# Summing Strassen-Winograd products over 128 partitions instead of 64, in a gated feed-forward layer behind polysketch attention

## The chip, the cores and the metric

The kernel runs on one core of one Trainium2 chip. A core has TensorE (PE: matrix products; PEld in a profile is its loading of weights), VectorE (DVE), ScalarE (ACT), GpSimd (POOL) and SyncE (SP), which here only issues transfers. The metric is the device time of one execution, in microseconds (us); lower is better. All data are float32. The matrices come in as float64, seen by the kernel as pairs of 32-bit words, and are narrowed to float32 on the chip.

## What is computed

```python
def phi(x):                      # q, k, v: (4, 4, 1088, 32); S1, S2: (8, 32)
    a = np.einsum('rd,bhsd->bhsr', S1, x)
    b = np.einsum('rd,bhsd->bhsr', S2, x)
    return np.einsum('bhsi,bhsj->bhsij', a, b).reshape(*x.shape[:-1], 64)
q_p, k_p = phi(q), phi(k)
kv = np.einsum('bhsf,bhsd->bhfd', k_p, v)
z = np.sum(k_p, axis=2)
x = einsum('bhsf,bhfd->bhsd', q_p, kv) / (einsum('bhsf,bhf->bhs', q_p, z)[..., None] + 1e-6)
x = x.transpose(0, 2, 1, 3).reshape(4352, 128)
gate = 1.0 / (1.0 + np.exp(-(x @ w_gate)))      # w_gate, w_val: (128, 1536)
out = (gate * (x @ w_val)) @ w_out              # w_out: (1536, 128)
```

## The kernel before

The 4352 tokens of the feed-forward layer are cut into nine chunks: eight of 512 tokens (0 to 7) and one of 256 (chunk 8). A chunk takes twelve *waves* (chunk 8 takes six, each of two column blocks of 256 tokens). A wave, `w1`, multiplies 128 columns of `w_gate` and of `w_val` with the chunk's tokens into a double PSUM buffer `wave` (two of them in turn), and issues ScalarE's sigmoid (`sg`). The product of the two halves, `g`, is VectorE's `glu`; it is emitted at the start of the next wave's turn. The instructions' order on each engine is the order in which the Python code emits them.

One turn of the loop in `slot` is called a *slot* here: `glu` of the wave before, then one piece of work from the list `moe["late"]`, then all products with `w_out` whose due slot (`todo`) has come, then the next wave with its sigmoid. Attention for batches 1 to 3 is spread between the slots by a plan written out by hand (`plan`), so that its steps (`turn_k`, `turn_q`, `begin`, `outer`, `sum_z`, `kv_all`, `qmult`, `ndt`, `weights_z`, `parts`) come at numbered waves; batch 0 runs at the start of the kernel, with `warm` products on constants between its steps to fill TensorE. `begin` ends with transfers that spread a small matrix `cq` over partitions by way of DRAM (`dq`); `parts` needs what they bring (`denj` reads `b` and others).

Chunk 0 and chunk 8 multiply with `w_out` plainly (`w2`, `w2_end`, output tile `moeout`). Chunks 1 to 7 (`fast`) use a scheme of seven products for each 2 x 2 block product: two neighbouring waves are a pair; the blocks are two column blocks of the pair by two halves of 256 tokens (`HALF`), against two row blocks of `w_out` by two halves of 64 output columns. GpSimd makes four differences of `g` for each pair (`token_sums`, tile `tsum`, `t[0]` to `t[3]`; `t[0]` after the even wave, the other three after the odd one), and weight sums `ws` once (`weight_sums`). Each of the seven products has 64 output rows and 256 columns, so two lie side by side on the 128 columns of TensorE's array: `lo` (output partitions 0 to 63) and `hi` (64 to 127). `w2_a` issues four of the seven into the PSUM bank `acc0`, `w2_b` three into `acc1`, each accumulated over the chunk's six pairs. `w2_a` is due three slots after the pair's odd wave, `w2_b` four; the last pair of chunk 7 one slot sooner (`early`).

After the sixth pair the seven accumulated products are combined into the chunk's 128 x 512 output. They lie on both halves of the partitions[...]; so ScalarE copies the `hi` half of a bank to partitions 0 to 63 (tile `other`, variable `e`), and VectorE sums on 64 partitions into `res` (variable `r`). The first copy and sum follow the last `w2_a` at once (L473, L475); the other sums, two transposes of 64 x 512 (L514) and the store are pieces of `moe["late"]`, one a slot (two a slot in chunk 8). `store` issues its four or more transfers on SP. `acc0` and `acc1` have one buffer each: the next chunk's first product into a bank waits until all readers of the old sums are through. `w2_end` uses `acc0` for the last chunk's output, and `store_end` copies that to two `o_end` tiles which share the two buffers of `o_sb`.

Of the kernel before, what the change touches and what calls it, by code (L numbers as in the profile page):

```python
# [8 lines left out]
F32 = mybir.dt.float32  # L9
# [3 lines left out]
ALU = mybir.AluOpType  # L13
# [3 lines left out]
P = 128  # L17
# [3 lines left out]
def kernel(  # L21
# [12 lines left out]
    nc = tc.nc  # L34
# [6 lines left out]
    NJ = DFF // P  # L41
# [7 lines left out]
    TCH = 512  # L49
    tok_chk = [(o, min(TCH, NTOK - o)) for o in range(0, NTOK, TCH)]  # L50
# [3 lines left out]
    sbA = ctx.enter_context(tc.tile_pool(name="sbA", bufs=2))  # L54
# [131 lines left out]
    HALF = TCH // 2  # L186
# [157 lines left out]

    xT = const.tile([P, NTOK], F32, tag="xT")

    moe = {"sum": -1, "ci": 0, "w": 0, "n": 0, "ready": 0, "acc": None, "gate": None, "todo": [], "late": []}

    def fast(ci):
        return 0 < ci < len(tok_chk) - 1 and tok_chk[ci][1] == TCH  # L350
# [14 lines left out]
    def token_sums(g, t, odd):  # L365
        def sub(u, in0, in1):
            nc.gpsimd.tensor_tensor(out=t[:, u], in0=in0, in1=in1, op=ALU.subtract)  # L367

        if not odd:
            sub(0, g[:, 0, HALF:], g[:, 0, :HALF])  # L370
            return
        sub(2, g[:, 1, HALF:], t[:, 0])
        sub(3, t[:, 2], g[:, 1, :HALF])
        sub(1, g[:, 1, HALF:], g[:, 0, HALF:])

    def product(out, lhsT, rhs, start, stop):
        nc.tensor.matmul(  # L377
            out=out, lhsT=lhsT, rhs=rhs, start=start, stop=stop, skip_group_check=True
        )
# [34 lines left out]
    def w2(ci, j0, jn, g):  # L414
        if j0 == 0:
            moe["sum"] = ci
            moe["acc"] = pso.tile([P, TCH], F32, tag="acc0", name="moeout")
        for jj in range(jn):
            j = j0 + jj
            for d in (slice(0, P),) if j < NJ - 2 else (slice(0, 64), slice(64, P)):  # L420
                nc.tensor.matmul(  # L421
                    out=moe["acc"][d],
                    lhsT=w_sb[:, 2, j, d],
                    rhs=g[:, jj],
                    start=(j == 0),
                    stop=(j == NJ - 1),
                )
        if j0 + jn == NJ:
            o_sb = sbA.tile([P, 2, TCH // 32, 32], F32, tag="o_sb", name="o_sb")[:, 0]
# [27 lines left out]

    fst = {}

    def w2_a(ci, i, g, t):  # L460
        if i == 0:
            moe["sum"] = ci
            fst["a"] = pso.tile([P, TCH], F32, tag="acc0", name="prod")
        lo, hi = fst["a"][:64], fst["a"][64:]
# [12 lines left out]

    def add(out, in0, in1, op=ALU.add):
        nc.vector.tensor_tensor(out=out, in0=in0, in1=in1, op=op)  # L479

    def twice(x):
        return bass.AP(tensor=x.tensor, offset=x.offset, ap=[list(x.ap[0]), [0, 2], [1, HALF]])

    def ends(r, u, step):
        x = r[:, u]
        return bass.AP(
            tensor=x.tensor, offset=x.offset, ap=[list(x.ap[0]), [step * HALF, 2], [1, HALF]]
        )

    def w2_b(ci, i, g, t):  # L490
        if i == 0:
            fst["b"] = pso.tile([P, TCH], F32, tag="acc1", name="prod")
        lo, hi = fst["b"][:64], fst["b"][64:]
        w, first, last = w_sb[:, 2], i == 0, i == NJ // 2 - 1
        p5 = (lo[:, :HALF], ws[:, 0, i], t[:, 0], first, last)
        p4 = (hi[:, :HALF], w[:, 2 * i + 1, 64:], t[:, 3], first, last)
        p7 = ((hi if i % 2 else lo)[:, HALF:], ws[:, 2, i], t[:, 1], False, i >= NJ // 2 - 2)
        for p in (p4, p5, p7) if i % 2 else (p5, p4, p7):
            product(*p)
        if last:  # L500
            e, r = fst["e"], fst["r"]
            nc.scalar.copy(out=e[:, 1], in_=hi.rearrange("p (u x) -> p u x", u=2))
            o_sb = sbA.tile([P, 2, TCH // 32, 32], F32, tag="o_sb", name="o_sb")

            def fifth_seventh():
                add(ends(r, 2, 3), twice(lo[:, :HALF]), ends(r, 2, 2))
                add(r[:, 0], lo[:, HALF:], e[:, 1, 1])

            def last_sums():
                add(r[:, 3], r[:, 4], e[:, 1, 0], op=ALU.subtract)  # L510
                add(r[:, 3:5], ends(r, 3, 2), twice(r[:, 0]))

            def turned(d):
                nc.vector.transpose(  # L514
                    out=o_sb[:64, d].rearrange("p t x -> p (t x)"),
                    in_=r[:, 1 + 2 * d : 3 + 2 * d].rearrange("p u x -> p (u x)"),
                )

            def turn_store():
                turned(1)  # L520
                store(ci, lambda g4: o_sb[32 * (g4 % 2) : 32 * (g4 % 2) + 32, g4 // 2])

            moe["late"] += [fifth_seventh, last_sums, lambda: turned(0), turn_store]

    def w1():

# [45 lines left out]
        def glu():  # L572
            g = pair[:, odd]
            todo = moe["todo"]
            if jn == 2:
                nc.vector.tensor_tensor(  # L576
                    out=g.rearrange("p (j u s y) -> p j y u s", j=2, u=2, y=4),
                    in0=wv[:, 1].rearrange("p (j y u s) -> p j y u s", j=2, u=2, y=4),
                    in1=sg.rearrange("p (j y u s) -> p j y u s", j=2, u=2, y=4),
                    op=MUL,  # L580
                )
            else:
                nc.vector.tensor_tensor(out=g, in0=wv[:, 1], in1=sg, op=MUL)  # L583
            if not fast(ci):
                lag = 4 if ci else 2
                part = (ci, j0, jn, g.rearrange("p (j t) -> p j t", j=jn))
                todo.append((n + lag, lambda: (w2_end if ci else w2)(*part)))
                return
            if not odd:
                moe["t"] = raw.tile([P, 4, HALF], F32, tag="w_in", name="tsum")  # L590
            token_sums(pair, moe["t"], odd)
            if odd:
                part = (ci, j0 // 2, pair, moe["t"])
                early = ci == len(tok_chk) - 2 and j0 == NJ - 1
                todo.append((n + 3 - early, lambda: w2_a(*part)))
                todo.append((n + 4 - early, lambda: w2_b(*part)))

        moe["gate"] = glu
        moe["w"] += 1
# [10 lines left out]
    def slot(group, waves, behind=None):  # L610

        if group is not None:
            group()
        todo = moe["todo"]
        for _ in range(waves):
            more = moe["ci"] < len(tok_chk)
            if more and sum(tok_chk[moe["ci"]]) > moe["ready"]:
                break
            glu()
            for _ in range(2 if moe["ci"] >= len(tok_chk) - 1 else 1):  # L620
                if moe["late"]:
# [781 lines left out]
```

## Time and profile before

| | us |
|---|---|
| median of 3 runs (lowest, highest) | 292.83 (292.31, 293.69) |
| the profiled execution: its own time | 296.02 |
| its span, first to last instruction | 294.1 |
| TensorE busy, share of the span | 288.8, 98% |
| VectorE busy | 186.5, 63% |
| ScalarE busy | 93.7, 32% |
| GpSimd busy | 160.6, 55% |

The page of a profile gives busy times, groups of equal instructions by source line with their mean duration, and the chain of work that ended last. Further views are used here: the timeline (start and length in us, engine, line, operation, tile written and tiles read, shapes), tables of busy time by stretches of the span, and a list of waits. An item `[1.11 <-PE wave L540]` says that the engine had been idle for 1.11 us before the instruction and that TensorE's work of line 540 ended this. A float32 matrix product is recorded as two passes, so counts of matmuls are twice those in the code. Most lines of the profile are those of small helpers: L377 is every one of the seven products, L367 every difference on GpSimd, L479 every sum on VectorE.

### The profile page before, as it was taken

To read this page: it belongs to the slowest core of one execution; us is meant where nothing else is said; L and a number is where in the kernel's file an instruction comes from. 1 tells how busy PE (TensorE), PEld (TensorE's weight loads), DVE (VectorE), ACT (ScalarE), POOL (GpSimd) and SP (SyncE) were. 2 spreads that over 40 slices of the span, in tenths; PEclk is the share of its full clock that TensorE was granted. 3 is DMA by queue.
4 is the path that set the end of the run, shared out by engine and by line. 5 is a ranking of instruction groups with operands and counts; after the bars stand their busy time and mean duration, and the time that the engine had idled before them with its cause. 6 is when DMAs were issued, how large, how long until landed. Compare 5 with 4: busy or idle time off the path is not lost.

```text
span 294.1 us, 5762 instructions
## 1 busy us (share of the span) xinstructions
PE 288.8 (98%) x2264; PEld 156.6 (53%) x2264; DVE 186.5 (63%) x316; ACT 93.7 (32%) x172; POOL 160.6 (55%) x222
## 2 busy tenths in 40 slices
PE   8989999999999999999999999999999999999995
PEld 3543433355455455545555555554555555555895
DVE  5778789885656766677556696667436423552482
ACT  3386542321324222323224222323223223322321
POOL 2266544796535657655456498555456565646300
PEclk9999999999999999999999999999999999999999
DMA  7993613295640168416000474202000200020003
GB/s 219 347 336 68 150 39 125 74 180 137 186 97 0 19 163 159 133 50 177 12 0 2 129 174 106 37 0 38 1 0 2 36 2 0 0 31 7 0 4 54
DMA packets 28890, 24.23 MB, mean 82 GB/s; under 512 B 18560, under 2 KB 24064, under 8 KB 28864
## 3 DMA queue, kind: packets, MB, share of 16 engines
q1 hardware_dynamic: 25808, 21.95, 30.1%
q10 hardware_dynamic: 3056, 1.92, 2.3%
q8 instruction: 18, 0.29, 0.4%
q14 instruction: 8, 0.07, 0.1%
HBM read 20.60 MB, written 3.26 MB: 81 GB/s over the span
## 4 chain that ended last, share of the span: by engine, by line
PE 89%; DMA 7%; SPq 1%; DVE 0%; issue 0%; ACT 0%; DVEq 0%
PE wave L540 55%; PE prod L377 20%; DMA bq<-dq 5%; PE moeout L421 4%; PE moeout L447 2%; PE warm L297 1%; PE kps L673 1%; SPq L844 1%; PE nps L1258 1%; DMA s_in<-in_S_dram 1%; PE kvz L892 1%; PE cqps L819 1%; DMA dq<-cq 1%; DMA b<-dq 1%; PE denj L1021 0%; PE dps L1063 0%
## 5 line engine op out<-in xcount | busy, mean ns | idle before, releaser
L540 PE MATMUL wave<-xT,w_sb 128*64 128x512 f32 (+3 forms) x820 | 210.6, 566 | 0.0
L540 PEld LDWEIGHTS wave<-xT,w_sb 128*64 128x64 f32 (+1 forms) x820 | 85.4, 140 | 63.2 <-issue 51.0
L548 ACT ACTIVATE sg<-wave 128x512 f32<-128x512 f32 x102 | 60.9, 597 | 171.1 <-PE wave L540 163.2
L583 DVE TENSOR_TENSOR g<-wave,sg 128x512 f32<-128x512 f32 x96 | 65.9, 686 | 76.3 <-ACT sg L548 75.0
L367 POOL TENSOR_TENSOR tsum<-g 128x256 f32<-128x256 f32 x84 | 67.9, 810 | 29.7 <-DVE g L583 29.6
L367 POOL TENSOR_TENSOR tsum<-g,tsum 128x256 f32<-128x256 f32 x42 | 34.2, 814 | 57.8 <-DVE g L583 57.6
L377 PE MATMUL prod<-tsum,ws 128*64 128x256 f32 x252 | 62.8, 381 | 0.0
L377 PEld LDWEIGHTS prod<-tsum,ws 128*64 128x64 f32 x252 | 31.2, 137 | 16.0 <-issue 11.8
L377 PE MATMUL prod<-g,w_sb 128*64 128x256 f32 x168 | 34.7, 381 | 0.0
L367 POOL TENSOR_TENSOR tsum<-tsum,g 128x256 f32<-128x256 f32 x42 | 32.7, 779 | 3.3
L377 PE MATMUL prod<-tsum,w_sb 128*64 128x256 f32 x84 | 25.3, 383 | 0.0
L377 PEld LDWEIGHTS prod<-g,w_sb 128*64 128x64 f32 x168 | 16.0, 136 | 17.5 <-issue 14.7
L377 PE MATMUL prod<-g,ws 128*64 128x256 f32 x84 | 25.0, 379 | 0.0
L117 POOL TENSOR_TENSOR head<-head,tail 128x384 int32<-128x384 int32 (+1 forms) x10 | 9.9, 987 | 13.9 <-DVE head L111 12.6
L377 PEld LDWEIGHTS prod<-g,ws 128*64 128x64 f32 x84 | 11.5, 137 | 3.7
L421 PE MATMUL moeout<-g,w_sb 128*128 128x512 f32 (+1 forms) x28 | 12.5, 603 | 0.0
L377 PEld LDWEIGHTS prod<-tsum,w_sb 128*64 128x64 f32 x84 | 10.8, 137 | 3.0 <-issue 2.2
L872 DVE TENSOR_TENSOR qp<-qp,bq 128x1152 f32<-128x1152 f32 (+1 forms) x7 | 9.4, 1344 | 4.6 <-DMA a<-dq 4.6
L752 DVE TENSOR_TENSOR kp<-kab 128x1152 f32<-128x1152 f32 (+2 forms) x10 | 10.9, 1101 | 0.0
L576 DVE TENSOR_TENSOR g<-wave,sg 128x512 f32<-128x512 f32 x6 | 6.7, 1121 | 4.6 <-ACT sg L548 4.6
L479 DVE TENSOR_TENSOR res<-prod,other 64x512 f32<-64x512 f32 (+1 forms) x14 | 7.6, 544 | 3.1 <-DMA a<-dq 1.6
L514 DVE STREAM_TRANSPOSE o_sb<-res 64x512 f32<-64x512 f32 x14 | 9.6, 688 | 0.0
(129 smaller groups left out, 209.6 us busy)
## 6 DMA issues: line engine op xcount, KB each, us to landing
qp<-dq SPq DMA_DIRECT2D x7, 576.0 KB
bq<-dq SPq DMA_DIRECT2D x14, 288.0 KB
kq<-in_k_dram SPq DMA_DIRECT2D x3, 544.0 KB
kq<-in_q_dram SPq DMA_DIRECT2D x3, 544.0 KB
w_in<-in_moe_w_out_dram SPq DMA_DIRECT2D x6, 256.0 KB
w_in<-in_moe_w_gate_dram SPq DMA_DIRECT2D x5, 256.0 KB
w_in<-in_moe_w_val_dram SPq DMA_DIRECT2D x5, 256.0 KB
v<-in_v_dram SPq DMA_DIRECT2D x8, 144.0 KB
```

The lines of the kernel that those rows point to most:

```text
L117: nc.gpsimd.tensor_tensor(out=head, in0=head, in1=tail, op=ALU.add)
L367: nc.gpsimd.tensor_tensor(out=t[:, u], in0=in0, in1=in1, op=ALU.subtract)
L377: nc.tensor.matmul(out=out, lhsT=lhsT, rhs=rhs, start=start, stop=stop, skip_group_check=True)
L421: nc.tensor.matmul(out=moe["acc"][d], lhsT=w_sb[:, 2, j, d], rhs=g[:, jj], start=(j == 0), stop=(j == NJ - 1),)
L479: nc.vector.tensor_tensor(out=out, in0=in0, in1=in1, op=op)
L514: nc.vector.transpose(out=o_sb[:64, d].rearrange("p t x -> p (t x)"), in_=r[:, 1 + 2 * d : 3 + 2 * d].rearrange("p u x -> p (u x)"),)
L540: nc.tensor.matmul(out=wv[d, which, jj * tw + o : jj * tw + o + tp], lhsT=w_sb[:, which, j0 + jj, d], rhs=xT[:, t0 + o : t0 + o + tp], sta ...
L548: nc.scalar.activation(out=sg, in_=wv[:, 0], func=ACTF.Sigmoid)
L576: nc.vector.tensor_tensor(out=g.rearrange("p (j u s y) -> p j y u s", j=2, u=2, y=4), in0=wv[:, 1].rearrange("p (j y u s) -> p j y u s", j ...
L583: nc.vector.tensor_tensor(out=g, in0=wv[:, 1], in1=sg, op=MUL)
L752: eng.tensor_tensor(out=KP[b][:, pi, j0:j1].rearrange("p j m (i l) -> p (j m) i l", i=R), in0=bass.AP(tensor=a0.tensor, offset=a0.offset, ...
L872: nc.vector.tensor_tensor(out=q0, in0=q0, in1=half(BQ[b], n), op=MUL)
```

## The change

- The seven products are dealt out anew. `w2_a` takes `t[2]` and `t[1]` in place of one product on `g` and of one on `t[2]`; the product of `g` with the second row block moves to `w2_b`. The signs and the order of GpSimd's differences are changed to suit.
- The sums run over 128 partitions. ScalarE makes seven copies of 64 x 256 for each chunk instead of two of 64 x 512, in both directions between the halves (`cross`). They are put on a list, `moe["copies"]`, and emitted in `slot` behind the next wave, hence behind its sigmoid. Six read PSUM; one reads a sum, `r[64:, 0]`.
- VectorE makes five sums (four of 128 x 256, one of 64 x 256) and one transpose of 128 x 512 for each chunk. All of them are late pieces: first `shared`, with the two sums that read `acc0` (the second reads the first's result), a slot after the last `w2_a`; then `first_half`, one sum, and `turn_store`, which stores.
- The first pair of chunk 1 has its `w2_a` and `w2_b` due one slot later (`behind`); the last pair of chunk 7 is no longer due one sooner.
- The warm product behind the transpose of the sketches, at the start of the kernel, has 128 columns instead of 64. `o_sb` is half as large.

```diff
         sub(2, g[:, 1, HALF:], t[:, 0])
-        sub(3, t[:, 2], g[:, 1, :HALF])
         sub(1, g[:, 1, HALF:], g[:, 0, HALF:])
+        sub(3, g[:, 1, :HALF], t[:, 2])
...
     def w2_a(ci, i, g, t):
...
         product(lo[:, :HALF], w[:, 2 * i, :64], g[:, 0, :HALF], first, last)
-        product(hi[:, :HALF], w[:, 2 * i + 1, :64], g[:, 1, :HALF], first, last)
+        product(hi[:, :HALF], ws[:, 1, i], t[:, 2], first, last)
         product(lo[:, HALF:], ws[:, 3, i], g[:, 1, HALF:], False, last)
-        product(hi[:, HALF:], ws[:, 1, i], t[:, 2], False, last)
+        product(hi[:, HALF:], ws[:, 2, i], t[:, 1], False, last)
         if last:
-            e = fst["e"] = raw.tile([P, 2, 2, HALF], F32, tag="w_in", name="other")[:64]
-            r = fst["r"] = raw.tile([P, 6, HALF], F32, tag="w_in", name="res")[:64]
-            nc.scalar.copy(out=e[:, 0], in_=hi.rearrange("p (u x) -> p u x", u=2))
-
-            add(ends(r, 1, 3), twice(lo[:, :HALF]), e[:, 0])
-            moe["late"] += [lambda: add(r[:, 2], lo[:, HALF:], r[:, 4])]
+            e = fst["e"] = raw.tile([P, 4, HALF], F32, tag="w_in", name="other")
+            r = fst["r"] = raw.tile([P, 3, HALF], F32, tag="w_in", name="res")
+            cross(e[:64, 0], hi[:, :HALF])
+            cross(e[64:, 0], lo[:, :HALF])
+            cross(e[:64, 1], lo[:, :HALF])
+
+            def shared():
+                add(r[:, 0], ps[:, :HALF], e[:, 0])
+                add(r[:, 0], ps[:, HALF:], r[:, 0])
+                cross(e[64:, 1], r[64:, 0])
+
+            moe["late"] += [shared]
+
+    def cross(out, in_):
+        moe["copies"].append(lambda: nc.scalar.copy(out=out, in_=in_))
...
     def w2_b(ci, i, g, t):
...
-        p5 = (lo[:, :HALF], ws[:, 0, i], t[:, 0], first, last)
+        p5 = (lo[:, HALF:], ws[:, 0, i], t[:, 0], False, last)
         p4 = (hi[:, :HALF], w[:, 2 * i + 1, 64:], t[:, 3], first, last)
-        p7 = ((hi if i % 2 else lo)[:, HALF:], ws[:, 2, i], t[:, 1], False, i >= NJ // 2 - 2)
-        for p in (p4, p5, p7) if i % 2 else (p5, p4, p7):
+        out2 = hi[:, HALF:] if i % 2 else lo[:, :HALF]
+        p2 = (out2, w[:, 2 * i + 1, :64], g[:, 1, :HALF], first, i >= NJ // 2 - 2)
+        for p in (p4, p5, p2) if i % 2 else (p2, p4, p5):
             product(*p)
         if last:
             e, r = fst["e"], fst["r"]
-            nc.scalar.copy(out=e[:, 1], in_=hi.rearrange("p (u x) -> p u x", u=2))
...
-            moe["late"] += [fifth_seventh, last_sums, lambda: turned(0), turn_store]
+            cross(e[:64, 2], lo[:, HALF:])
+            cross(e[64:, 2], lo[:, HALF:])
+            cross(e[:64, 3], hi[:, HALF:])
+            o_sb = sbA.tile([P, TCH // 32, 32], F32, tag="o_sb", name="o_sb")
+
+            def first_half():
+                add(r[:, 1], ps[:, :HALF], e[:, 1])
+                add(r[:64, 1], r[:64, 1], e[:64, 3])
+
+            def turn_store():
+                nc.vector.transpose(
+                    out=o_sb.rearrange("p t x -> p (t x)"),
+                    in_=r[:, 1:3].rearrange("p u x -> p (u x)"),
+                )
+                store(ci, lambda g4: o_sb[32 * g4 : 32 * g4 + 32])
+
+            moe["late"] += [first_half, lambda: add(r[:, 2], r[:, 0], e[:, 2]), turn_store]
...
-                early = ci == len(tok_chk) - 2 and j0 == NJ - 1
-                todo.append((n + 3 - early, lambda: w2_a(*part)))
-                todo.append((n + 4 - early, lambda: w2_b(*part)))
+                behind = ci == 1 and j0 == 1
+                todo.append((n + 3 + behind, lambda: w2_a(*part)))
+                todo.append((n + 4 + behind, lambda: w2_b(*part)))
...
             if more:
                 w1()
-            elif not todo:
+            for copy in moe["copies"]:
+                copy()
+            moe["copies"] = []
+            if more:
+                continue
+            if not todo:
                 break
             else:
                 todo.pop(0)[1]()
...
-    warm(64)
+    warm(128)
```

More of the change, by code (lines that the diff above doesn't have):

```diff
@@ L345 @@
     xT = const.tile([P, NTOK], F32, tag="xT")
-    moe = {"sum": -1, "ci": 0, "w": 0, "n": 0, "ready": 0, "acc": None, "gate": None, "todo": [], "late": []}
+    moe = {"sum": -1, "ci": 0, "w": 0, "n": 0, "ready": 0, "acc": None, "gate": None, "todo": [], "late": [], "copies": []}
     def fast(ci):
@@ L428, in w2 @@
         if j0 + jn == NJ:
-            o_sb = sbA.tile([P, 2, TCH // 32, 32], F32, tag="o_sb", name="o_sb")[:, 0]
+            o_sb = sbA.tile([P, TCH // 32, 32], F32, tag="o_sb", name="o_sb")
             nc.vector.transpose(out=o_sb.rearrange("p t d -> p (t d)"), in_=moe["acc"])
@@ L463, in w2_a, with add @@
             fst["a"] = pso.tile([P, TCH], F32, tag="acc0", name="prod")
-        lo, hi = fst["a"][:64], fst["a"][64:]
+        ps = fst["a"]
+        lo, hi = ps[:64], ps[64:]
         w, first, last = w_sb[:, 2], i == 0, i == NJ // 2 - 1
         product(lo[:, :HALF], w[:, 2 * i, :64], g[:, 0, :HALF], first, last)
-        product(hi[:, :HALF], w[:, 2 * i + 1, :64], g[:, 1, :HALF], first, last)
+        product(hi[:, :HALF], ws[:, 1, i], t[:, 2], first, last)
         product(lo[:, HALF:], ws[:, 3, i], g[:, 1, HALF:], False, last)
-        product(hi[:, HALF:], ws[:, 1, i], t[:, 2], False, last)
+        product(hi[:, HALF:], ws[:, 2, i], t[:, 1], False, last)
         if last:
-            e = fst["e"] = raw.tile([P, 2, 2, HALF], F32, tag="w_in", name="other")[:64]
-            r = fst["r"] = raw.tile([P, 6, HALF], F32, tag="w_in", name="res")[:64]
-            nc.scalar.copy(out=e[:, 0], in_=hi.rearrange("p (u x) -> p u x", u=2))
-            add(ends(r, 1, 3), twice(lo[:, :HALF]), e[:, 0])
-            moe["late"] += [lambda: add(r[:, 2], lo[:, HALF:], r[:, 4])]
[L478 to L488, printed above, removed]
+            e = fst["e"] = raw.tile([P, 4, HALF], F32, tag="w_in", name="other")
[10 more added lines that the diff above has]
+        moe["copies"].append(lambda: nc.scalar.copy(out=out, in_=in_))
+    def add(out, in0, in1):
+        nc.vector.tensor_tensor(out=out, in0=in0, in1=in1, op=ALU.add)
     def w2_b(ci, i, g, t):
@@ L492, in w2_b @@
             fst["b"] = pso.tile([P, TCH], F32, tag="acc1", name="prod")
-        lo, hi = fst["b"][:64], fst["b"][64:]
+        ps = fst["b"]
+        lo, hi = ps[:64], ps[64:]
         w, first, last = w_sb[:, 2], i == 0, i == NJ // 2 - 1
-        p5 = (lo[:, :HALF], ws[:, 0, i], t[:, 0], first, last)
+        p5 = (lo[:, HALF:], ws[:, 0, i], t[:, 0], False, last)
         p4 = (hi[:, :HALF], w[:, 2 * i + 1, 64:], t[:, 3], first, last)
-        p7 = ((hi if i % 2 else lo)[:, HALF:], ws[:, 2, i], t[:, 1], False, i >= NJ // 2 - 2)
-        for p in (p4, p5, p7) if i % 2 else (p5, p4, p7):
+        out2 = hi[:, HALF:] if i % 2 else lo[:, :HALF]
+        p2 = (out2, w[:, 2 * i + 1, :64], g[:, 1, :HALF], first, i >= NJ // 2 - 2)
+        for p in (p4, p5, p2) if i % 2 else (p2, p4, p5):
             product(*p)
@@ L501, in w2_b @@
             e, r = fst["e"], fst["r"]
[L502 to L513, printed above, removed]
+            cross(e[:64, 2], lo[:, HALF:])
+            cross(e[64:, 2], lo[:, HALF:])
+            cross(e[:64, 3], hi[:, HALF:])
+            o_sb = sbA.tile([P, TCH // 32, 32], F32, tag="o_sb", name="o_sb")
+            def first_half():
+                add(r[:, 1], ps[:, :HALF], e[:, 1])
+                add(r[:64, 1], r[:64, 1], e[:64, 3])
+            def turn_store():
                 nc.vector.transpose(
-                    out=o_sb[:64, d].rearrange("p t x -> p (t x)"),
-                    in_=r[:, 1 + 2 * d : 3 + 2 * d].rearrange("p u x -> p (u x)"),
-                )
-            def turn_store():
-                turned(1)
-                store(ci, lambda g4: o_sb[32 * (g4 % 2) : 32 * (g4 % 2) + 32, g4 // 2])
-            moe["late"] += [fifth_seventh, last_sums, lambda: turned(0), turn_store]
+                    out=o_sb.rearrange("p t x -> p (t x)"),
+                    in_=r[:, 1:3].rearrange("p u x -> p (u x)"),
+                )
+                store(ci, lambda g4: o_sb[32 * g4 : 32 * g4 + 32])
+            moe["late"] += [first_half, lambda: add(r[:, 2], r[:, 0], e[:, 2]), turn_store]
     def w1():
```

## Prediction

> **What bounds the kernel now.** I read the page's first part, then the table by stages, then the list of waits, then the timeline at a change of chunk. From the page:
>
> ```profile
> PE 288.8 (98%) x2264; PEld 156.6 (53%) x2264; DVE 186.5 (63%) x316; ACT 93.7 (32%) x172; POOL 160.6 (55%) x222
> ```
>
> TensorE is busy nearly throughout. Busy need not be peak, so I checked rates: in the chain of waits a wave takes 1.72 us, `w2_a`'s four products 0.86, and two pairs of waves with their products take 9.88 us (from the wave at 255.68 to the one at 265.56), 4.94 each. The parts sum to that: a 64-column product of 512 elements costs 0.43 us of half the array, so 16 wave halves of 0.43 plus 14 of 0.215 over two halves are 4.95. Nothing is lost between chunks either. The table by stages (columns: length, then the busy time of each engine, TensorE first):
>
> ```profile
> 17.40:50.00 32.60, 32.60 (x111) 14.21 (x112) 27.68 (x54) 17.48 (x35) 18.79 (x26) 1.00 0.49 131
> 50.00:80.00 30.00, 29.55 (x308) 13.43 (x306) 22.20 (x36) 8.15 (x14) 20.87 (x27) 1.00 0.56 130
> 80.00:276.00 196.00, 196.00 (x1473) 107.99 (x1471) 114.62 (x180) 56.16 (x95) 115.89 (x150) 1.00 0.23 53
> 276.00:294.10 18.10, 14.90 (x186) 13.63 (x182) 10.40 (x15) 4.42 (x8) 0.00 (x1) 0.98 0.13 24
> ```
>
> From 80 to 276 us, the fast chunks, TensorE is busy 196.00 of 196.00. The list of waits has nothing of those chunks but one transfer in chunk 1:
>
> ```profile
> PE denj L1021 <- DMA b<-dq: 0.4, 1, 0.4
> ```
>
> So work taken off VectorE, ScalarE or GpSimd there gains nothing; what can happen is that TensorE starts to wait. The place is the change of chunk. This is the timeline at the last one of the plain chunks (start, length, engine, line, out<-in; from a longer answer):
>
> ```profile
> 250.26 0.60 ACT L548 ACTIVATE sg<-wave 128x512 f32<-128x512 f32 x1 [1.11 <-PE wave L540]
> ...
> 250.89 0.58 ACT L502 COPY other<-prod 64x512 f32<-64x512 f32 x1
> 250.96 0.69 DVE L583 TENSOR_TENSOR g<-wave,sg 128x512 f32<-128x512 f32 x1 [1.09 <-ACT sg L548]
> 251.57 0.41 DVE L479 TENSOR_TENSOR res<-prod,res 64x256 f32<-64x256 f32 x1
> ...
> 252.20 0.65 PE L377 MATMUL prod<-g,w_sb 128*64 128x256 f32 x4
> ```
>
> L479 at 251.57 is the last reader of bank `acc0` (the "late" sum behind `glu`); it ends at 251.98. At 252.20 the next chunk's first product overwrites that bank. The margin is **0.22 us**.
>
> [...] In the built program of the changed kernel the first full-width sum therefore waits for the third ScalarE copy out of `acc0`, not just for the two it uses. The trace of before agrees as far as it goes: the copy of `acc0` ends at 249.15 and the sum on that bank starts at 249.19; but that sum also needs the copy's result[...]. [...] the warm product of 512 columns at 11.29 us takes 0.99 us for each of its two passes, a 512-column wave on the full array after 17 us about 0.43. [...] `glu` at 58.61 starts only as the outer product before it ends.
>
> **The change, part by part.**
>
> Products. Seven of 256 columns per pair as before, moved between `w2_a` and `w2_b`, halves alternating as before: 0 us. `w2_a` now needs the second of the three odd GpSimd differences (`t[1]`) instead of the first. From the timeline that second difference ends 1.53 us before `w2_a` starts in plain pairs, and 0.21 us before it in the worst pair (173.96 against 174.17); the fourth product, which reads it, is 0.43 us later. No wait: 0. `w2_b` now reads `g` too; a `g` buffer is written again two slots later, so 0.
>
> VectorE. Per chunk before: one 64x512 sum at 0.68, the late ones 0.41, 0.67, 0.41, 0.41 and 0.98, two transposes of 0.69: 4.9 us. After: five sums of 256 columns at about 0.41 and one transpose of 0.69 (a 128x512 one, L430, takes 0.705): 2.75. Saves 2.2 us per chunk beside a full TensorE: 0 on the path.
>
> ScalarE. Before, two copies of 0.58; after, seven of 64x256. A 128x256 copy (L914) takes 0.372; two 128x512 copies of 0.588 (L790) take 1.07 together, so one begins 0.1 before the other ends, and a 256 copy follows the next after 0.27. The first three lie behind the sigmoid of `w2_a`'s slot, four behind the next: 3 x 0.27 + 0.6 and 4 x 0.27 + 0.6, under 1.8 us, in slots of 2.4 to 2.6 us. No later sigmoid is late: 0.
>
> **The hand-over of `acc0`** is where it goes. Times of the stretch above, with S = 250.86, the sigmoid's end. Copies start at S - 0.10 (as `nd` at 124.52 behind the sigmoid ending at 124.62) and the third ends 0.54 + 0.37 later, S + 0.81. The first sum starts at S + 0.88 (0.04 to 0.10 from ScalarE to VectorE in the rows above), takes 0.41; the second reads its result, starts 0.03 later (256.36 + 0.41 to 256.80) and takes 0.41; from VectorE's end to TensorE's start are 0.06 us (17.31 to 17.37). So the bank is free at S + 1.79 = 252.65, where TensorE wants it at 252.20: **a wait of 0.45 us**, during which every matmul queued behind that product stands. The same difference at the other changes, from their timelines (start of the product less the sigmoid's end): 1.33 at 93.15, 1.55 at 126.17, 1.33 at 158.16, 1.35 at 190.85, 1.33 at 222.44, giving 0.46, 0.24, 0.46, 0.44, 0.46. Six changes: 2.51 us. Seventh, chunk 8's first output product (281.99) takes `acc0` too. With `early` gone, `w2_a` of the last pair runs a slot later; the wave behind it ends at about 279.6 (277.0 + 0.86 + 1.72), its sigmoid at 280.45, `glu` takes 1.12 there and ends at 281.67, the sums end at 282.45, free at 282.51: 0.52. Sum **3.03 us**. From below: if copies cost no more than `glu`, the sums start right behind it and the bank is free at S + 1.62, 0.17 less at each of six: 2.0. From above: if 256-column copies don't overlap (0.37 apart), 0.2 to 0.3 more at each of seven: 5. I take 3.0.
>
> Bank `acc1`: its last copy ends at about 254.13, its sum at 254.61, free at 254.67, against `w2_b` at 254.84 + 0.45: 0.
>
> The extra slot for chunk 1's first pair. Four waves then stand back to back, and the fourth needs the buffer that `glu` releases at 59.29: it starts at 59.35 instead of 58.96, 0.39 lost. Then TensorE meets the `denj` wait (0.42 in the fence), whose transfer was sent at 54.60, ahead of all this. So it is swallowed: 0; if the cover fails, 0.39.
>
> warm(128): by the 512-column row (0.99 us a pass) 64 more columns are 0.12 us in each of two passes. The first lies within the 0.27 us from one pass's start to the next (5.68 to 5.95); `kps` (6.30) follows TensorE, since `sk` is done at 6.11: +0.1. Bounds: +0.25, or a gain (rival 2).
>
> Stores. One transpose instead of two; four issues on SP as before, one slot earlier in steady state, hence ahead of `begin(2)`'s spread in one case, 4 x 0.45 us against a copy that lands 2.1 us after its issue: 0. At the end the store is issued later: transpose ends at 287.35 + 0.52, last issue 1.44 later, and it lands 2.0 after that, 290.8 + 0.52. `o_end`'s second copy reuses that buffer and starts at 290.94 + 0.52: just 0.1 us to spare, 0 to 0.3.
>
> **Sum.** 2.51 + 0.52 + 0.1 = 3.1 us. The profiled execution took 296.02 (span 294.1 and 1.9 around it), which gives 299.1; it is 3.2 us slower than the median of 292.83 in runs without a profile. The difference carries over: **295.9 us**, 1.1% more.
>
> **Rivals.**
> 1. *The hand-over hides*: copies end earlier than I chain them, or TensorE has loaded weights and catches up. For it: the margin before was 0.22 us, so only 0.3 us per change needs to go. Against: 196.00 of 196.00 leaves nothing to catch up with, and of the 1.33 us from S to the product `glu` takes 0.10 + 0.69, which leaves 0.54 for two dependent sums of 0.41. 0 to 1.4 us: 292.8 to 294.2.
> 2. *The clock opens earlier* thanks to the extra warm columns (ends faster). [...] in the trace full speed comes at about 13.6 (`dps` passes 0.38, then 0.20). [...]
> 3. *More waits*: copies not overlapping, GpSimd late near 174 or 191 us, the swallowed 0.39 not swallowed, the last buffer late: +4 to +5, 296.8 to 297.8.
>
> **How the numbers follow.** My forecast (294.8 to 296.8) 0.58, rival 3 0.20, rival 1 0.16, rival 2 deciding 0.06. Slower by over 0.5% (1.46 us, about what a measurement of this kernel can tell from no change) is 0.78, same 0.16, faster 0.06. The range leaves out rival 2's gain and part of rival 1 below, and the end of rival 3 above: 292.9 to 297.6.
>
> **What would show it.** In the profile after: TensorE waits for VectorE's full-width sum at six changes of chunk, 0.2 to 0.5 us each, and before chunk 8's first `moeout`; between 80 and 276 us busy falls below the stretch by about 2.5 us; VectorE's busy time falls by about 15 us, ScalarE's rises by about 10; the `denj` wait shrinks to about 0. It is wrong if no product waits for VectorE at a change of chunk, or if the fast chunks are as long as before and the start differs.

## The result, and the profile after

The changed kernel takes **300.54 us** (median of 6 runs, 299.94 to 301.01) against 292.68 us for the kernel before in the same comparison (6 runs): a ratio of **1.0263**, 95% interval 1.0241 to 1.0285. It is 7.9 us slower. The forecast was 295.9 us with a range up to 297.6: the direction was right, the size was less than half of what came.

The profiled execution of the changed kernel took 300.9 us, its span is 299.1. The busy times of its page:

```profile
PE 286.6 (96%) x2264; PEld 155.6 (52%) x2264; DVE 175.3 (59%) x302; ACT 103.8 (35%) x207; POOL 162.1 (54%) x222
```

VectorE has lost 11.2 us of work against the profile that the prediction used, ScalarE has gained 10.1, and TensorE's busy time has hardly moved, in a span that is 5.0 us longer. The table by stages (length, then the busy time of each engine, TensorE first) says where TensorE now stands still:

```profile
80.00:276.00 196.00, 192.99 (x1443) 105.75 (x1441) 102.06 (x164) 63.54 (x123) 113.49 (x146) 1.00 0.21 49
276.00:299.10 23.10, 16.95 (x203) 14.51 (x199) 9.46 (x13) 6.45 (x14) 1.71 (x3) 0.98 0.10 19
```

The stretch from 80 to 276 us, 196.00 of 196.00 before, has lost 3.0 us, and the last stage is longer. The same table of a second profile of the unchanged kernel, taken later (its span is 291.0):

```profile
80.00:276.00 196.00, 196.00 (x1485) 109.83 (x1483) 113.28 (x177) 56.99 (x97) 115.19 (x148) 1.00 0.22 49
276.00:291.00 15.00, 11.75 (x157) 10.86 (x153) 8.62 (x13) 3.01 (x6) 0.00 (x0) 0.99 0.15 27
```

In the list of waits of the changed kernel (engine and line, what it waited for: us in total, times, longest) these are new or grown:

```profile
PE prod L377 <- ACT sg L550: 2.6, 4, 0.7
PE moeout L447 <- ACT sg L550: 0.6, 1, 0.6
DVE res L493 <- ACT other L490: 8.0, 13, 0.9
DVE o_end L403 <- DMA out_dram<-o_end: 3.9, 1, 3.9
```

The first two name the sigmoid; the timeline at the change from chunk 6 to chunk 7 shows what the product really waits for (start, length, engine, line, out<-in, and what ended the idle time before it):

```profile
251.28 0.60 ACT L550 ACTIVATE sg<-wave 128x512 f32<-128x512 f32 x1 [2.00 <-PE prod L377]
...
251.90 1.12 ACT L490 COPY other<-prod 64x256 f32<-64x256 f32 x3
...
251.98 0.69 DVE L585 TENSOR_TENSOR g<-wave,sg 128x512 f32<-128x512 f32 x1 [1.98 <-ACT sg L550]
...
253.05 0.42 DVE L493 TENSOR_TENSOR res<-prod,other 128x256 f32<-128x256 f32 x1 [0.39 <-ACT other L490]
253.47 0.60 ACT L550 ACTIVATE sg<-wave 128x512 f32<-128x512 f32 x1 [0.45 <-PE wave L542]
253.51 0.42 DVE L493 TENSOR_TENSOR res<-prod,res 128x256 f32<-128x256 f32 x1
254.05 0.13 PEld L377 LDWEIGHTS prod<-g,w_sb 128*64 128x64 f32 x1 [1.50 <-ACT sg L550]
254.09 0.40 PE L377 MATMUL prod<-g,w_sb 128*64 128x256 f32 x1 [0.65 <-ACT sg L550]
```

The sigmoid ends at S = 251.88. Three copies follow one behind the other, 1.12 us; the first sum starts 0.03 us after the third, the second 0.03 after the first and ends at 253.94; then the next chunk's first product goes into `acc0`, at S + 2.21, 0.15 us after that sum's end. The distance of 0.15 from the second sum's end is the same at all seven places. The next sigmoid, at 253.47, ends just before the product too, at 254.07, but the product's weights (PEld) were on their way at 254.05, and at the first two changes no sigmoid ends between S and the product. In the kernel before the product went in at S + 1.33. The last entry of the list of waits is at the end of the span:

```profile
293.19 0.27 ACT L403 COPY o_end<-moeout 128x128 f32<-128x128 f32 x1 [2.38 <-DMA out_dram<-o_sb]
293.48 0.62 ACTq L405 DMA_DIRECT2D out_dram<-o_end  x1
295.89 0.29 DVE L403 COPY o_end<-moeout 128x128 f32<-128x128 f32 x1 [3.94 <-DMA out_dram<-o_end]
```

VectorE's copy of the second output tile starts 2.7 us after ScalarE's copy of the first, when the first tile's transfer has landed. In the built program both `o_end` tiles now stand at one address (133088); before they stood at two (133088 and 137184).

With the second profile of the kernel before as the base, the spans' difference of 8.1 us divides like this. The first product of chunk 2 comes at 91.69 against 90.01: 0.88 of it is the first wait, 0.80 the start (in the profiles below, the start without waits scatters by as much). From there to the first product of chunk 8 it is 192.98 against 188.83 us: 4.15 for the six other waits. By the table below these are 5.0 us longer than in the kernel before; 0.8 of that takes the place of waits for `acc1` that the kernel before has there (experiment 2). From there to the end it is 14.43 against 12.16: 2.27 for the late tile.

### The profile page after: what moved, and what is told of

The parts are those of the page before. It is cut to its first block, busy times and chain, and to the rows that moved or that the text cites. A ratio compares the mean times of both kernels' runs of the same rounds, so it can differ in the third digit from the quotient of the medians.

```text
span 299.1 us, 5779 instructions
## 1 busy us (share of the span) xinstructions
PE 286.6 (96%) x2264; PEld 155.6 (52%) x2264; DVE 175.3 (59%) x302; ACT 103.8 (35%) x207; POOL 162.1 (54%) x222
## 4 chain that ended last, share of the span: by engine, by line
PE 89%; DMA 3%; DVE 3%; ACT 3%; issue 1%; SPq 1%; DVEq 0%; ACTq 0%
PE wave L542 57%; PE prod L377 21%; PE moeout L421 4%; DMA kq<-in_q_dram 2%; ACT sg L550 2%; PE kvz L899 1%; PE nps L1265 1%; ACT other L490 1%; PE cqps L826 1%; DMA out_dram<-o_end 1%; PE kps L680 1%; DMA out_dram<-o_sb 1%; DVE res L493 1%; DVE kp L759 1%; PE nps L1089 0%
## 5 line engine op out<-in xcount | busy, mean ns | idle before, releaser
L585 DVE TENSOR_TENSOR g<-wave,sg 128x512 f32<-128x512 f32 x96 | 66.0, 688 | 84.4 <-ACT sg L550 84.0
L367 POOL TENSOR_TENSOR tsum<-g,tsum 128x256 f32<-128x256 f32 x84 | 70.0, 833 | 58.5 <-DVE g L585 58.4
L377 PE MATMUL prod<-tsum,ws 128*64 128x256 f32 x252 | 68.3, 382 | 0.0
L377 PE MATMUL prod<-g,w_sb 128*64 128x256 f32 x168 | 50.3, 381 | 3.0 <-ACT sg L550 2.6
L377 PEld LDWEIGHTS prod<-g,w_sb 128*64 128x64 f32 x168 | 22.1, 137 | 29.5 <-issue 22.3
L377 PEld LDWEIGHTS prod<-tsum,ws 128*64 128x64 f32 x252 | 32.0, 136 | 8.7 <-issue 5.9
L490 ACT COPY other<-prod 64x256 f32<-64x256 f32 x42 | 15.4, 366 | 0.6
L759 DVE TENSOR_TENSOR kp<-kab 128x1152 f32<-128x1152 f32 (+2 forms) x10 | 11.2, 1132 | 0.0
L493 DVE TENSOR_TENSOR res<-prod,other 128x256 f32<-128x256 f32 x14 | 5.9, 424 | 8.0 <-ACT other L490 8.0
L297 PE MATMUL warm<-const-float32-1.0 128*128 128x512 f32 (+2 forms) x12 | 6.6, 670 | 0.8 <-PEq L1394 0.8
```

The source lines that it names most:

```text
L377: nc.tensor.matmul(out=out, lhsT=lhsT, rhs=rhs, start=start, stop=stop, skip_group_check=True)
L490: moe["copies"].append(lambda: nc.scalar.copy(out=out, in_=in_))
L493: nc.vector.tensor_tensor(out=out, in0=in0, in1=in1, op=ALU.add)
L759: eng.tensor_tensor(out=KP[b][:, pi, j0:j1].rearrange("p j m (i l) -> p (j m) i l", i=R), in0=bass.AP(tensor=a0.tensor, offset=a0.offset, ...
```

## The experiments

S is the end of the sigmoid in the slot of a chunk's last `w2_a`. When the next chunk's first product into `acc0` starts, read from the timelines of single profiles at the seven changes of chunk:

| kernel | chunks 1 to 2, 2 to 3, ... 6 to 7 | into chunk 8 | time, us |
|---|---|---|---|
| before (second profile) | S + 1.33, 1.55, 1.33, 1.35, 1.33, 1.33 | no wait | 292.72 |
| changed | S + 2.21 at all six | S + 2.21 | 300.54 |
| copies at once | S + 1.73 at all six | S + 2.06 | 298.61 |
| copies and sums at once | S + 1.33, 1.55, 1.33, 1.33, 1.33, 1.33 | S + 1.34 | 294.87 |
| third copy from SBUF | S + 1.83 at all six | S + 2.09 | 298.50 |
| copies straight down | S + 1.88 at all six | S + 2.11 | 298.86 |
| third copy first | S + 2.07 at all six | S + 2.09 | 299.47 |
| output tiles apart | S + 2.21 at all six | S + 2.21 | 297.94 |
| last slot given back | S + 2.21 at all six | no wait | 297.17 |
| both repairs | S + 1.33, 1.55, 1.33, 1.33, 1.33, 1.33 | S + 1.34 | 292.57 |

The kernel before, run beside each group, had medians from 292.6 to 293.3 us.

### 1. The kernel before, profiled again

No edit.

> The kernel before, unchanged, profiled a second time. My theory: the profiled execution that the prediction was built on (span 294.1, own time 296.0) opened TensorE's full clock late, so its start was about 1.9 us longer than in the profile of the changed kernel; a second profile then shows a span of 291 to 292.5 with the first wave at 15.5 to 16, and the time without a profile is 292.3 to 293.7 again. Rival (profiling itself costs this kernel 3 us): span 294 again, first wave near 17.4. In either case TensorE is busy 196.0 of 196.0 in the fast chunks.

Measured: 292.72 us (292.09 to 293.66, 20 runs), ratio 1.000 (0.999 to 1.001). This profiled execution took 292.79 us, span 291.0, first wave at 14.98 instead of 17.37; the warm product of 512 columns ahead of `dps` takes 1.11 us for its two passes (at 9.45) instead of 2.06 (at 11.29). So this profile is no slower than the runs without one; the execution that the prediction read was a late one. The wait of `denj` for a transfer, which the prediction quoted from it, is not in this profile.

### 2. Copies at once

```diff
-            cross(e[:64, 0], hi[:, :HALF])       # on the list: behind the next sigmoid
-            cross(e[64:, 0], lo[:, :HALF])
-            cross(e[:64, 1], lo[:, :HALF])
+            nc.scalar.copy(out=e[:64, 0], in_=hi[:, :HALF])     # at once
+            nc.scalar.copy(out=e[64:, 0], in_=lo[:, :HALF])
+            nc.scalar.copy(out=e[:64, 1], in_=lo[:, :HALF])
```

> The changed kernel, with the three ScalarE copies out of acc0 issued as soon as the bank's last product is, ahead of the next sigmoid; the two sums stay behind the next slot's work. Theory 1 (the hand-over of acc0 holds the next product up by 0.87 us at seven places, because three copies of 0.37 stand behind the sigmoid and two sums behind those): the copies are done before the sigmoid, so the first sum starts right behind glu; bank free at about S + 0.71 + 0.42 + 0.04 + 0.42 + 0.16 = S + 1.75 against 1.33 wanted, a wait of 0.4 instead of 0.87 at each of seven: 3.0 to 3.5 us faster than the changed kernel, 297.2 us. Theory 2 (the hand-over's price lies in the two sums alone, the copies being hidden): no change, 300.5. Theory 3 (the 7.9 us come from the order of products, the extra slot or the warm columns): no change, 300.5.

Measured: 298.61 us (298.20 to 299.07), 1.9 us faster than the changed kernel. Its timeline at the same change (S = 249.85):

```profile
248.32 0.37 ACT L480 COPY other<-prod 64x256 f32<-64x256 f32 x1
...
249.95 0.69 DVE L585 TENSOR_TENSOR g<-wave,sg 128x512 f32<-128x512 f32 x1 [1.98 <-ACT sg L550]
...
250.56 0.41 DVE L493 TENSOR_TENSOR res<-prod,other 128x256 f32<-128x256 f32 x1
...
251.58 0.40 PE L377 MATMUL prod<-g,w_sb 128*64 128x256 f32 x1 [0.17 <-DVE res L493]
```

The copies are over before the sigmoid; the first sum stands right behind `glu` (L585), the second ends at 251.43, and the bank is free at S + 1.73 where S + 1.75 was expected. Theories 2 and 3 fall: the copies are not hidden, and they are a part of the cost. The gain is smaller than expected for two reasons. At chunk 8 `glu` itself takes 1.1 us and binds, S + 2.06. And at the first two changes the next product, into the other bank, `acc1`, now waits for the sum that frees that bank:

```profile
126.47 0.42 DVE L493 TENSOR_TENSOR res<-prod,other 128x256 f32<-128x256 f32 x1 [0.87 <-ACT other L490]
...
127.04 0.40 PE L377 MATMUL prod<-g,w_sb 128*64 128x256 f32 x1 [0.22 <-DVE res L493]
```

It comes 2.94 and 3.22 us after the chunk's first product, in the changed kernel 2.60 and 2.74; that takes back 0.34 and 0.49 us. The kernel before waits at `acc1` too, although its table has TensorE busy for 196.00 of 196.00 us. In its second profile:

```profile
125.50 0.41 DVE L479 TENSOR_TENSOR res<-prod,other 64x256 f32<-64x256 f32 x1
...
126.05 0.40 PE L377 MATMUL prod<-tsum,ws 128*64 128x256 f32 x1
```

This product starts 0.15 us after the sum's end and 3.03 us after the chunk's first product. Where the bank is free in time it comes after 2.58 (the last two changes of experiment 3), which is the 0.86 of `w2_a` and the 1.72 of a wave. So the kernel before loses 0.38 and 0.45 us at the first two changes and about 0.06 at the last three, 1.0 in all.

### 3. Copies and sums at once

```diff
+            (the three copies at once, as in experiment 2)
-            moe["late"] += [shared]
+            shared()
```

> The changed kernel, with the three copies out of acc0 and the two sums on it all issued at once, ahead of the next sigmoid and the next glu. Theory 1 (hand-over of acc0): the bank is free about 2 us before the next chunk's first product wants it, TensorE waits nowhere at a change of chunk and is busy 196.0 of 196.0 again; 5.5 to 6 us faster than the changed kernel, 294.7 us. It could cost something where glu stands behind the two sums (0.84 us): then the wait names glu, and 1 to 2 us of the gain are missing. Theory 3 (order of products, extra slot, warm columns): 300.5, unchanged.

Measured: 294.87 us (294.65 to 295.16), **5.7 us faster** than the changed kernel; ratio to the kernel before 1.0074 (1.0050 to 1.0097). The timeline at the change (S = 247.85) and the table's row of the fast chunks:

```profile
246.32 0.37 ACT L480 COPY other<-prod 64x256 f32<-64x256 f32 x1
...
246.72 0.42 DVE L493 TENSOR_TENSOR res<-prod,other 128x256 f32<-128x256 f32 x1 [0.74 <-ACT other L480]
...
247.18 0.42 DVE L493 TENSOR_TENSOR res<-prod,res 128x256 f32<-128x256 f32 x1
...
249.18 0.38 PE L377 MATMUL prod<-g,w_sb 128*64 128x256 f32 x1
```

```profile
80.00:276.00 196.00, 196.00 (x1487) 111.74 (x1485) 103.72 (x166) 64.95 (x127) 113.79 (x148) 1.00 0.22 49
```

The sums lie ahead of `glu`, which does not come late for it; the product comes at S + 1.33 as in the kernel before, and TensorE is busy 196.00 of 196.00. Everything of the change but the time at which these copies and sums are issued is still in this kernel, so that time costs 5.7 us, 0.81 on average at seven places. By the waits for `acc0` alone it would be 5.9; but this kernel waits longer for `acc1` at the first two changes than the changed one (the product comes after 2.84 and 2.91 us, against 2.60 and 2.74).

### 4. The output tiles in buffers of their own

```diff
-        o_sb = [sbA.tile([P, P], F32, tag="o_sb", name="o_end") for _ in range(2)]
+        o_sb = [sbA.tile([P, P], F32, tag="o_end", name="o_end") for _ in range(2)]
```

> The changed kernel, with the two output tiles of the last chunk in buffers of their own. My theory: in the changed kernel both share one buffer, so the second copy waits for the first one's transfer to land (2.4 us from 293.5 to 295.9); apart, VectorE's copy starts at about 293.6 and the kernel is 2.3 us faster, 298.2 us, the seven waits at the changes of chunk unchanged. Rival (the end is set by the second transfer's own landing and by the drain behind it, which start no earlier): under 0.5 us faster, 300.2.

Measured: 297.94 us (297.68 to 298.35), **2.6 us faster** than the changed kernel. The end of its timeline:

```profile
292.92 0.27 ACT L403 COPY o_end<-moeout 128x128 f32<-128x128 f32 x1 [2.38 <-PE moeout L447]
...
293.35 0.29 DVE L403 COPY o_end<-moeout 128x128 f32<-128x128 f32 x1 [1.68 <-PE moeout L447]
```

VectorE's copy starts 0.43 us after ScalarE's, released by TensorE; in the changed kernel it was 2.7. So the second transfer goes out 2.3 us earlier. The seven waits are as they were. The rival falls: the landing of the second transfer moves with its issue.

### 5. Both repairs together

The edits of experiments 3 and 4.

> The changed kernel with both repairs: copies and sums of acc0 issued at once, and the two last output tiles in buffers of their own. My theory (the seven hand-overs and the shared buffer are the whole of the 7.9 us): 294.87 less 2.6 is 292.3, that is within 0.5 us of the kernel before; TensorE busy 196.0 of 196.0 in the fast chunks and no wait of VectorE's last copy for a transfer. Rival (something else of the change costs up to 1 us: the warm columns, the extra slot, the order of products): 293 to 293.6. Against a gain over the kernel before: 11 us less VectorE work lie beside a full TensorE, so nothing of it shows.

Measured: 292.57 us (22 runs, median), ratio 1.0002 (0.9987 to 1.0018). The two causes are the whole of the difference; what is left of the change, the new order of products, the extra slot, the warm columns and 12 us less VectorE work, comes to nothing that can be measured:

```profile
80.00:276.00 196.00, 196.00 (x1489) 112.14 (x1487) 103.32 (x164) 65.24 (x128) 113.69 (x148) 1.00 0.22 49
```

In the traces two small terms cancel. From the first product of chunk 2 to that of chunk 8 it is 188.47 us here and 188.83 in the second profile of before, since `acc1` is free a little sooner (at the first two changes its product comes after 2.84 and 2.90 us, against 2.96 and 3.03). The extra slot costs about as much (experiment 6).

### 6. The due times alone

```diff
 (the kernel before)
-                early = ci == len(tok_chk) - 2 and j0 == NJ - 1
+                early = -(ci == 1 and j0 == 1)
```

> The kernel before with the due times of the changed kernel alone: one slot more for the first pair of chunk 1, none taken from the last pair. The prediction had this at 0 for the first (a fourth wave held up by 0.39 us, swallowed by the wait of denj for its transfer) and let the store at the end come one slot later: 292.6 us. Rival A (the transfer of denj is not late in usual executions, so nothing swallows the 0.39): 293.0. Rival B (the late store at the end collides with the last output tiles): 293 to 295.

Measured: 295.75 us (295.31 to 296.15), ratio 1.0099 (1.0081 to 1.0117): 2.9 us slower: rival B, with rival A beside it. The chunk's first output product and the end, from its timeline (the sigmoid before the product ended at 277.83):

```profile
279.43 1.09 PE L447 MATMUL moeout<-w_sb,g 128*64 128x128 f32 x16
...
287.94 0.27 ACT L403 COPY o_end<-moeout 128x128 f32<-128x128 f32 x1 [2.44 <-DMA out_dram<-o_sb]
...
290.64 0.29 DVE L403 COPY o_end<-moeout 128x128 f32<-128x128 f32 x1 [3.99 <-DMA out_dram<-o_end]
```

The product starts at S + 1.60 (0.26 of waiting against 1.34), and VectorE's copy waits for the first tile's transfer exactly as in the changed kernel: 2.7 us after ScalarE's, which is 2.3 more than in experiment 4. So with the old sums too, and with the larger `o_sb`, losing the last pair's early slot is enough to put both tiles into one buffer. The two make 2.5 us. The rest, 0.4, is the extra slot, rival A: from the wave at 52.46 us to the first product of chunk 2 it is 37.89 us here, and 37.51 in the second profile of before (from the wave at 52.50).

### 7. The last slot given back

```diff
 (the changed kernel)
-                behind = ci == 1 and j0 == 1
+                behind = (ci == 1 and j0 == 1) - (ci == len(tok_chk) - 2 and j0 == NJ - 1)
```

> The changed kernel with the slot given back that the kernel before took from the last pair of the last fast chunk. Theory 1 (that slot decides both the hand-over of acc0 to chunk 8 and which buffer the second output tile gets, as the due times alone cost the kernel before 2.9 us): the last pair's sums end a slot earlier, so the wait of 0.87 us at chunk 8 goes and the output tiles stand in two buffers; the six waits at the other changes stay: 300.5 less 2.6 less 0.9, 297.0 us. Theory 2 (the shared buffer comes from the smaller o_sb tile, not from the slot): the last wait at chunk 8 goes, the shared buffer stays: 299.6 us.

Measured: 297.17 us (297.00 to 298.30), 3.4 us faster than the changed kernel, theory 1. The end:

```profile
291.87 0.27 ACT L403 COPY o_end<-moeout 128x128 f32<-128x128 f32 x1 [2.44 <-PE moeout L447]
...
292.31 0.29 DVE L403 COPY o_end<-moeout 128x128 f32<-128x128 f32 x1 [1.70 <-PE moeout L447]
```

The tiles stand apart again, and chunk 8 does not wait for `acc0`. Leaving out `early`, one small edit, is 3.4 of the 7.9 us: the shared buffer and the wait before chunk 8. By what rule the pool chooses the buffer is open.

### 8. The third copy from SBUF

```diff
 (the changed kernel)
-            cross(e[:64, 1], lo[:, :HALF])
+            cross(e[:64, 1], xT[:64, :HALF])
```

> The changed kernel with the third of the three copies reading SBUF (a part of xT) in place of acc0: the same ScalarE work at the same place, but the first sum no longer has to wait for it; the term that this copy carries is left out of the result. Theory 1 (the three copies stand one behind the other at 0.376 us and the first sum waits for the third, because it touches the same bank): the first sum starts 0.37 us earlier at six changes of chunk (at chunk 8 the long glu binds instead), the waits there fall from 0.87 to 0.5: 2.2 us faster than the changed kernel, 298.3 us. Theory 2 (the first sum waits for something else, glu or the second copy, and the third copy runs beside it): no change, 300.5.

Measured: 298.50 us (298.38 to 298.66), 2.0 us faster than the changed kernel; theory 1. Its timeline (S = 250.08):

```profile
250.10 0.74 ACT L490 COPY other<-prod 64x256 f32<-64x256 f32 x2
...
250.18 0.69 DVE L585 TENSOR_TENSOR g<-wave,sg 128x512 f32<-128x512 f32 x1 [1.98 <-ACT sg L550]
...
250.87 0.40 ACT L490 COPY other<-xT 64x256 f32<-64x256 f32 x1
250.88 0.42 DVE L493 TENSOR_TENSOR res<-prod,other 128x256 f32<-128x256 f32 x1
...
251.91 0.40 PE L377 MATMUL prod<-g,w_sb 128*64 128x256 f32 x1 [0.28 <-DVE res L493]
```

The first sum now starts at 250.88, beside the third copy, and the bank is free at S + 1.83, 0.38 sooner: the time from one copy to the next. In the changed kernel that sum waits for a copy whose result it does not use. What is shown here is that the program orders the sum behind this copy out of its bank, and the price, 0.38 us at six changes of chunk; the reason for the order is not shown.

### 9. Straight copies, and another order: which of them overlap

```diff
 (the changed kernel; 9a)
-            cross(e[:64, 0], hi[:, :HALF])
-            cross(e[64:, 0], lo[:, :HALF])
-            cross(e[:64, 1], lo[:, :HALF])
+            cross(e[:, 0], ps[:, :HALF])
+            cross(e[:, 1], ps[:, HALF:])
+            cross(e[:, 3], ps[:, :HALF])
```

> The changed kernel with its three copies out of acc0 taken straight down, 128 x 256, no operand changing to the other half of the partitions: the same number of copies, elements per partition and places, the terms no longer crossing (what the copies carry is then not what the sums need, so this part of the computation is changed). It asks why the copies do not overlap. Theory 1 (a ScalarE instruction whose input or output starts in another half of the partitions than the one before it waits for that one's end; ones that stay overlap by 0.1 us, as the other rows of the trace do): the first copy starts 0.10 us before the sigmoid's end, the three follow at 0.27, the third ends at S + 0.81 as the prediction had it, the bank is free at about S + 1.87 in place of 2.21; six waits less by 0.34 and the one at chunk 8 by 0.1: 2.1 us faster than the changed kernel, 298.4 us. Theory 2 (copies out of one PSUM bank do not overlap, wherever they lie): spacing 0.38 and S + 2.21 again, 300.5 us.

```diff
 (the changed kernel; 9b)
+            cross(e[:64, 1], lo[:, :HALF])
             cross(e[:64, 0], hi[:, :HALF])
             cross(e[64:, 0], lo[:, :HALF])
-            cross(e[:64, 1], lo[:, :HALF])
```

> The changed kernel with the order of the three copies changed: the one that stays on the lower half (e[:64, 1] from lo) first, then the two that cross. Theory 1 (changing halves costs the overlap): behind the sigmoid, which stays on the lower half, this copy starts 0.10 us before the sigmoid's end, the two crossing ones follow without overlap, and all three end 0.12 us sooner; bank free at S + 2.09, six waits less by 0.12: 0.7 us faster than the changed kernel, 299.8 us. Theory 2 (no copy out of the bank overlaps): 300.5 us, first copy at S + 0.02.

Measured: 9a 298.86 us (298.48 to 298.95), 1.7 us faster than the changed kernel, where 2.1 was expected; 9b 299.47 us (299.17 to 299.67), 1.1 us faster, where 0.7 was expected. The copies of 9a (S = 250.27), then those of 9b (S = 250.73):

```profile
250.16 0.92 ACT L490 COPY other<-prod 128x256 f32<-128x256 f32 x3
```

```profile
250.63 1.11 ACT L490 COPY other<-prod 64x256 f32<-64x256 f32 x3
...
251.77 0.42 DVE L493 TENSOR_TENSOR res<-prod,other 128x256 f32<-128x256 f32 x1 [0.24 <-ACT other L490]
```

Straight copies start 0.10 us before the sigmoid's end and take 0.92 us for three; the bank is free at S + 1.88, where the prediction's own chain gives 1.79; the third copy ends at S + 0.82, and the prediction had 0.81. Part of the expected gain goes at `acc1`, as in experiment 2 (2.80 and 3.09 us, against 2.60 and 2.74). In 9b only the first, which stays on the lower half, starts 0.10 early; the two that cross follow without overlap, and the product comes at S + 2.07 (expected 2.09). Theory 2 falls in both: the bank and the number of copies are the same, and the copies that stayed on their half overlapped by 0.10 us, the others not. The copies of 9a are also twice as wide, 128 partitions; the first copy of 9b has 64, like those that cross, and overlaps all the same.

### 10. Two edits that were thought to cost nothing

```diff
 (the kernel before)
-    warm(64)
+    warm(128)
```

> The kernel before with 128 instead of 64 warm columns ahead of kps, nothing else. The prediction had this at +0.1 us (the first of two passes 0.12 us longer, kps behind it): 292.7. [...] Rival (the burst delays kps and what follows by more[...]): up to +0.5, 293.1.

Measured: 292.58 us (14 runs), ratio 0.9991 (0.9978 to 1.0004): no difference that shows, neither the 0.1 us expected nor a gain. That more warm columns bring full speed earlier, the prediction's rival 2, is not shown by any run here.

Both repairs with the last pair's slot given back, the edits of experiments 3, 4 and 7:

> Both repairs (copies and sums of acc0 issued at once, output tiles in buffers of their own) and the last pair's slot given back. My theory: after the repairs TensorE waits nowhere and the end is set by its last products and the last transfers, so an earlier sum of the last pair gains nothing: 292.5 us, as with the repairs alone and as the kernel before. Rival (the store of the last fast chunk, one slot earlier, leaves SP's queue and the DMA engines free for the last tiles): up to 0.5 us faster, 292.0.

Measured: 292.49 us (22 runs), ratio 0.9989 (0.9980 to 0.9997). It is the fastest kernel here, by 0.1%; the interval barely leaves out 1, so this is no sure gain.

## Why the prediction was right and wrong

**Right in the main: the bound.** A TensorE that is busy throughout from 80 to 276 us leaves next to nothing to gain (experiment 5: 12 us less VectorE work, time unchanged) and hardly any slack to absorb a wait. But "Nothing is lost between chunks either" was read from busy time, and that hid 1.0 us of waits for `acc1` (experiment 2). The product at 254.84, by which the prediction put `acc1` at 0, was itself held up by that bank's sum, and of the margin of 0.22 us at `acc0` the hand-over itself takes 0.15. **Right: the place.** The waits are where they were forecast, at six changes of chunk and before chunk 8's first `moeout`; `acc1` costs the changed kernel 0.13 us at one change, less than the kernel before. **Right: the products and the warm columns** at about 0 (experiments 5 and 10), and the 3.2 us by which the profile stood over the median (experiment 1). ScalarE's busy time rose by 10 as forecast; VectorE's fell by 11, not 15, off the path.

**Wrong in size: the chain behind S.** The prediction had the bank free at S + 1.79; it was S + 2.21.

| term | predicted | measured | difference |
|---|---|---|---|
| first copy starts | S - 0.10 | S + 0.02 | +0.12 |
| two spacings of copies | 2 x 0.27 | 2 x 0.38 | +0.22 |
| third copy's end to first sum | 0.07 | 0.03 | -0.04 |
| two sums and the step between | 0.85 | 0.88 | +0.03 |
| VectorE's end to TensorE's start | 0.06 | 0.15 | +0.09 |

That is 0.42 at each place, on top of 0.45, and in the last place 0.87 in all where 0.52 was forecast. The waits by the table sum to 5.9 us (0.88, 0.66, 0.88, 0.86, 0.88, 0.88, 0.87); 5.7 came out in experiment 3. Four fifths of the error, 0.34 of 0.42, come from one choice of row: the copies were priced by `nd` and L790, whose operands all start on the first partition, while the moved copies change halves. The fitting row stood in the prediction's own fence: the 64 x 512 copy of `hi` (L502) starts at 250.89, the sigmoid before it ended at 250.86. No overlap: at five changes of chunk in that profile this copy starts 0.02 to 0.03 us after a sigmoid's end, while `nd` behind a sigmoid starts 0.10 before it. The upper bound of 5 us took this case in, as rival 3, but the value chosen was the other one.

**Wrong: the buffer at the end.** "`o_end`'s second copy reuses that buffer", that of chunk 7's `o_sb`, "0 to 0.3". The copy did wait for a buffer, but for that of the other `o_end` tile, whose transfer is issued 0.3 us after ScalarE's copy and lands 2.4 us later: 2.3 us in the trace, 2.6 in experiment 4. The addresses of the two tiles stood in the built program and would have told it; the step took a turn of two buffers for granted. It was set off by the edit that the prediction treated only as a slot's delay of sums, `early` (experiments 6 and 7).

**Wrong in part: the extra slot.** It was put at 0, swallowed by the wait of `denj` for its transfer, and at 0.39 "if the cover fails". The second profile of before has no such wait of TensorE, and against it experiment 6 loses 0.38. So the cover is not there in every execution. That the term does not show in the time of experiment 5 is luck: the gain at `acc1`, which nobody forecast, is as large.

In sum: hand-over 5.7 in place of 3.0, the end 2.6 in place of 0 to 0.3, the rest near 0; 8.3 by the separate experiments, 7.9 by the result.

## What to carry to other kernels

Where the bounding engine has no slack, the reader that frees its buffer is the critical path: issue the copies and sums that release a bank ahead of the next slot's work, even if they then delay engines that have time (5.7 us here, experiment 3). Price a moved instruction by a row with the same partitions in and out, not only with the same shape (0.34 us a time here), and follow it to the start of the engine that waits. When an edit shifts issue order near shared buffers, look up which buffer each tile gets in the built program (2.6 us here). And a busy time equal to the stretch does not prove that nothing waits (196.00 of 196.00 hid 1.0 us here): compare the end of a bank's last reader with the start of the product that takes the bank.

## What the runs showed of the hardware

- **ScalarE's copies overlapped the instruction before them only where they stayed on the same half of the partitions.** The straight copies of 128 x 256 in 9a, and `e[:64, 1]` behind the sigmoid in 9b, started 0.10 us before the end of the instruction ahead of them, as `nd` did behind the sigmoid in the kernel before (0.10 at three places). The copies whose input or output lay on the other half than that of the instruction ahead of them started 0.01 to 0.03 us after its end, in the changed kernel in all 35 places behind a copy and all 14 behind a sigmoid. This was seen on ScalarE alone; no run here tests VectorE.
- **From VectorE's sum to the TensorE product that overwrote its bank: 0.15 us** wherever that sum was what the product waited for: at eight places of the changed kernel (seven at `acc0`, one at `acc1`) and six of the kernel before, in the profile that the prediction read (one at `acc0`, five at `acc1`), not the 0.06 of the row that the prediction took.
